# Another written-out order for an attention and feed-forward kernel, and its last output tile in parts of 384 and 128 columns

## The chip, the cores and the metric

The kernel runs on one NeuronCore of a Trainium2 chip. The metric is the device time of one execution in microseconds (us), as the median of several runs. One further execution is recorded by the hardware profiler; the lines and durations in this text come from it. The core has five engines that work side by side, each through its own queue in order: TensorE (PE; its weight loads are shown as PEld), VectorE (DVE), ScalarE (ACT), GpSimd (POOL) and SyncE (SP). DMA transfers are issued from the queues of POOL, SP and ScalarE.

## The reference

Attention over 8 batches and 8 heads, with 576 tokens and a head dimension of 64. In front of the keys and values stand 16 "beacon" keys and values which every query sees; the others are causal. Then a gated feed-forward network without a nonlinearity follows over all 4608 tokens:

```
scores = 0.125 * q @ concat(beacon_k, k).T      # masked above the diagonal
a      = exp(scores - max) / sum
x      = (a @ concat(beacon_v, v)) as 4608 tokens x 512
out    = ((x @ w1) * (x @ w2)) @ w3 @ w_out     # 512 -> 1024 -> 1024 -> 512
```

## The kernel before, in words

All products are in fp16 with fp32 sums. Since nothing nonlinear stands between `w3` and `w_out`, the kernel multiplies these two first (`Wt`, 1024 x 512) and so needs one output product instead of two.

There are no loops in the program that set the order of the work. A text, `ORDER`, lists every step; a short loop reads it and calls one small function for each entry. Each engine gets its instructions in the order of that list, and semaphores hold an instruction until its data is there and its buffer is free. So a step's place in the list is its place in the queue of its engine, and a step that waits holds everything behind it on that engine. The entries, with the lines of the profile:

- Loads, nearly all on POOL's queue (letter P; S is SP's queue, A is ScalarE's): `lq b c` and `lk b c` load queries and keys of batch b (chunk c of 128 rows; for batch 0, head pair c; lines 331, 339, 356), `lv` and `lvb` values and beacon values (339, 384), `lkb` beacon keys, `l1` and `l2` quarters of the two up-projections (389), `l3` an eighth of `w3` (398), `lo` a quarter of `w_out` (401). Up to eight loads are under way; a ninth waits for the oldest to land.
- Transposes of q and k: `tq`, `tk` on TensorE (421 for batch 0, 427 for others) with `eq`, `ek` copying the result out of PSUM; batch 0 first has its rows put in order by `cast`. Most of the later batches use transposing loads on SP instead, `Dq` and `Dk` (470, 476). `tn`, `en` do it for batch 0's beacon keys.
- The weight product: `t3 r` transposes an eighth of `w3` (483), `e3` copies it out, `f r a` multiplies (492), `ew` copies `Wt` out.
- Attention: `s b g` computes a group of score blocks (507; 13 groups a batch, K = 64 rows, two heads at once), `exp` exponentiates it on ScalarE (517, 128 x 1024, 1.03 us), `m` masks diagonal blocks on VectorE, `v b t h` multiplies with the values (538), `n` divides by the row sum on VectorE (549, 550).
- Turning x: `x b i` on TensorE (564) with the copy `ex`, or the transposing DMA `TX b i` on SP (573).
- Feed-forward, in 9 chunks of 512 tokens: `a mc kf` and `b mc kf` (579, four products of 512 columns each), copied or multiplied by `ea` and `eb`; `o mc mt` the output product of 128 tokens (600, eight products), `eo` scales it out of PSUM, `st` stores it (614).
- `spin n` runs n products of zeros on TensorE, to fill waits at the start. `consts` sets up constants.

A letter A or D in a copying step says whether ScalarE or VectorE does it; the number beside it is the PSUM bank. `o`, `eo` and `st` may carry a first column and a width, with which a tile is made in parts.

Two functions matter for the tail:

```
def eo(mc, mt, e, n, c0=0, w=DM):
    i = slot["st", (mc, mt)] if c0 else take("st", (mc, mt), NST)
    scaled(e, sts[i][:, ds(c0, w)], bank(n)[:, 0:w], float(1.0 / GS))
```

and `st`, which issues the store of these columns from the named queue. The whole order, before and after, is in the listing and in the diff.

Of the kernel before, what the change touches and what calls it, by code (L numbers as in the profile page):

```python
# [696 lines left out]
```

## Time and profile before

| | |
|---|---|
| median of 5 runs | 292.66 us (291.24 to 293.65) |
| the profiled execution | 292.49 us |
| its span, first to last instruction | 289.7 us |
| TensorE busy | 283.6 us (98%), 2904 matmuls |
| VectorE, ScalarE, POOL busy | 171.6, 147.3, 134.2 us |
| first matmul, first transpose, last matmul's end | 1.26, 5.99, 286.60 us |
| DMA moved | 38.85 MB, mean 134 GB/s |

The profile's page shows the busy time of each engine, the same in 40 slices of the span, the DMA queues, the chain of work that ended last, and the costliest groups of instructions with what ended the idle time before them. Other views of the trace show stages of the span, the chain in order of time, the waits, and the instructions in order of time. "Landing" is when a DMA's data is reported complete. A matmul is pipelined, so the price of one is read from start to start, not from its shown duration.

### The profile page before, as it was taken

How to read it: one execution, taken by the hardware profiler on the slowest of the kernel's cores; microseconds unless marked ns; L12 is line 12 of the kernel's file. 1: busy time of each engine (PE TensorE's matmuls, PEld its weight loads, DVE VectorE, ACT ScalarE, POOL GpSimd, SP SyncE). 2: the span in 40 equal slices, each digit the busy share in tenths (PEclk: the TensorE clock that was granted, in tenths of full speed). 3: DMA queues.
4: the chain of work that ended last, by engine and by line, in shares of the span. 5: the costliest groups of instructions: out<-in, count | busy, mean ns of one | idle time of the engine just before them, and what ended most of it. 6: DMA issues, size and time to landing. Idle time of an engine off the chain costs nothing.

```text
span 289.7 us, 7032 instructions
## 1 busy us (share of the span) xinstructions
PE 283.6 (98%) x2904; PEld 153.6 (53%) x2904; DVE 171.6 (59%) x370; ACT 147.3 (51%) x188; POOL 134.2 (46%) x187
## 2 busy tenths in 40 slices
PE   7999999999999999999999999999999999999995
PEld 3446675565565655565544555555555445444443
DVE  4244586885586856665563566575766565676710
ACT  3677779646574754678125656646473153000022
POOL 8769898798668651285396464450010011000000
PEclk9999999999999999999999999999999999999999
DMA  9999999999999999499999999997121005300033
GB/s 156 202 200 176 172 172 178 171 156 146 165 189 142 144 157 227 104 133 178 159 156 154 178 203 104 154 191 161 35 69 38 36 36 151 78 2 0 0 145 145
DMA packets 154318, 38.85 MB, mean 134 GB/s; under 512 B 144112, under 2 KB 150000, under 8 KB 154288
## 3 DMA queue, kind: packets, MB, share of 16 engines
q0 software_dynamic: 114800, 26.46, 104.7%
q1 hardware_dynamic: 39280, 11.68, 25.0%
q8 instruction: 22, 0.36, 0.5%
q10 hardware_dynamic: 208, 0.29, 0.4%
q14 instruction: 8, 0.07, 0.1%
HBM read 39.32 MB, written 9.44 MB: 168 GB/s over the span
## 4 chain that ended last, share of the span: by engine, by line
PE 86%; DMA 7%; POOL 5%; issue 1%; ACT 0%; POOLq 0%
PE one L579 44%; PE one L600 22%; PE one L538 10%; PE pair L507 8%; DMA q<-in_q_dram 2%; DMA st<-in_k_dram 2%; DMA wo<-in_moe_w_out_dram 2%; POOL va L339 2%; PE one L564 1%; POOL xT L398 1%; PE one L427 1%; POOL q L331 1%; PE one L492 1%; POOL k L339 1%; POOL w L389 0%
## 5 line engine op out<-in xcount | busy, mean ns | idle before, releaser
L579 PE MATMUL one<-xT,w 128*128 128x512 f16 x576 | 133.6, 379 | 0.0
L517 ACT ACTIVATE ring<-pair 128x1024 f16<-128x1024 f32 x104 | 99.3, 1028 | 21.2 <-PE pair L507 19.2
L579 PEld LDWEIGHTS <-w 128*128 128x128 f16 x576 | 53.0, 98 | 59.3 <-issue 2.7
L600 PE MATMUL one<-Wt,gT 128*128 128x512 f16 (+1 forms) x296 | 66.5, 374 | 0.0
L594 DVE TENSOR_TENSOR gT<-one,asb 128x512 f16<-128x512 f32 x72 | 49.1, 689 | 23.2 <-PE one L579 16.3
L299 ACT ACTIVATE asb<-one 128x512 f32<-128x512 f32 x32 | 19.2, 600 | 75.4 <-PE one L579 51.0
L614 POOL DMA_DIRECT2D out_dram<-st x27 | 15.3, 569 | 66.9 <-DVE st L301 29.6
L339 POOL DMA_DIRECT2D va<-in_v_dram x40 | 33.9, 851 | 21.8 <-PE one L538 15.6
L600 PEld LDWEIGHTS <-gT 128*128 128x128 f16 x296 | 27.7, 98 | 30.7 <-issue 1.3
L538 PEld LDWEIGHTS <-ring 128*128 128x128 f16 x960 | 35.2, 97 | 10.0 <-issue 1.0
L538 PE MATMUL one<-va,ring 128*128 128x65 f16 x960 | 37.8, 193 | 0.0
L301 DVE TENSOR_SCALAR asb<-one 128x512 f32<-128x512 f32 x40 | 27.5, 689 | 14.7 <-PE one L579 14.0
L339 POOL DMA_DIRECT2D k<-in_k_dram x35 | 29.8, 857 | 10.8 <-DMA kT<-k 6.7
L550 DVE TENSOR_TENSOR x<-one,rd 128x384 f16<-128x384 f32 (+1 forms) x64 | 31.4, 491 | 2.2
L331 POOL DMA_DIRECT2D q<-in_q_dram x35 | 30.0, 865 | 5.7 <-DMA va<-in_v_dram 3.1
L507 PE MATMUL pair<-qT,kT 64*128 64x80 f16 (+4 forms) x736 | 30.6, 225 | 0.1
L507 PEld LDWEIGHTS <-kT 64*128 64x128 f16 x736 | 19.7, 95 | 14.4 <-issue 11.9
L299 ACT ACTIVATE st<-one 128x512 f32<-128x512 f32 (+1 forms) x18 | 10.3, 574 | 24.3 <-PE one L600 23.9
L527 DVE TENSOR_TENSOR ring<-ring,MD 128x768 f16<-128x768 f16 x32 | 17.7, 552 | 7.9 <-ACT ring L517 7.9
L301 DVE TENSOR_SCALAR st<-one 128x512 f32<-128x512 f32 x19 | 13.1, 690 | 14.1 <-PE one L600 14.1
L527 DVE TENSOR_TENSOR ring<-ring,MX 128x384 f16<-128x384 f16 x32 | 11.3, 354 | 16.1 <-ACT ring L517 16.1
L549 DVE RECIPROCAL rd<-one 128x6 f32<-128x6 f32 (+1 forms) x64 | 11.7, 183 | 12.5 <-PE one L538 12.2
(63 smaller groups left out, 134.1 us busy)
## 6 DMA issues: line engine op xcount, KB each, us to landing
out_dram<-st POOLq DMA_DIRECT2D x27, 256.0 KB, 6.6
q<-in_q_dram POOLq DMA_DIRECT2D x28, 128.0 KB, 6.3
va<-in_v_dram POOLq DMA_DIRECT2D x24, 128.0 KB, 6.9
k<-in_k_dram POOLq DMA_DIRECT2D x21, 128.0 KB, 6.7
xT<-in_moe_w_dram POOLq DMA_DIRECT2D x8, 256.0 KB, 6.3
w<-in_moe_w_dram POOLq DMA_DIRECT2D x8, 256.0 KB, 7.3
out_dram<-st SPq DMA_DIRECT2D x8, 256.0 KB, 2.0
wo<-in_moe_w_out_dram POOLq DMA_DIRECT2D x4, 256.0 KB, 6.4
```

Of the source, the lines that this page charges most:

```text
L299: nc.scalar.activation(dst, src, AF.Copy, scale=by)
L301: nc.vector.tensor_scalar(dst, src, by, None, ALU.mult)
L331: nc.gpsimd.dma_start(dst[:rows, c], src[b, :, ds(c * P, rows), :].rearrange("h s d -> s h d"))
L339: nc.gpsimd.dma_start(dst[ds(p0, rows), c], src[b, :, ds(s0, rows), :].rearrange("h s d -> s h d"))
L507: nc.tensor.matmul(shape(n, "pair")[:, hh, ds(col, w)], kT[ds(hh * 64, 64), t, ts(jt, P)], qT[ds(hh * 64, 64), t, ds(q0, w)],)
L517: nc.scalar.activation(held(b, g)[:, :, 0:GW], shape(n, "pair"), AF.Exp, scale=scale)
L527: nc.vector.tensor_tensor(blk, blk, msk, ALU.mult)
L538: nc.tensor.matmul(pv[:, 2 * at + hh, 0 : D + 1], held(b, g)[:, hh, ds(col, P)], va[:, jt, 2 * t + hh, 0 : D + 1], start=(jt == 0), stop=( ...
L550: nc.vector.tensor_tensor(x16s[b % NB2][:, ds(2 * h, ni), ts(t, P)].rearrange("p i (h d) -> p i h d", h=2), pv[:, 0 : 2 * ni, 0:D].rearran ...
L579: nc.tensor.matmul(bank(n), w12[:, kt, ds(i * DF + kf * P, P)], xT[:, kt, ds(mc * 512, 512)], start=(kt == 0), stop=(kt == NKT - 1),)
L594: nc.vector.tensor_tensor(gTs[mc % 2][:, kf, :], bank(n), asb[slot["asb", (mc, kf)]], ALU.mult)
L600: nc.tensor.matmul(bank(n)[:, 0:w], gTs[mc % 2][:, kf, ts(mt, P)], Wt[:, kf, ds(c0, w)], start=(kf == 0), stop=(kf == NFT - 1),)
```

## The change

Only the text `ORDER` changes; all functions stay. 1190 entries become 1191. What differs:

- The first part, batch 0 and the weight product up to about the first scores of batch 1, is in another order: other eighths of `w3` first, scores after the first group later and products `f` earlier, the loads in an accordingly different order, other banks, and other choices between ScalarE and VectorE. The two loads outside POOL's queue swap queues.
- The rest has the same steps in a similar sequence, with differences in order, banks and engines throughout. In batch 7, tile 0 is turned by `x` and `ex` (TensorE, ScalarE) where it was a `TX` (SP). 22 output tiles instead of 19 are scaled by VectorE (with the last half tile's move among them), and 11 instead of 10 stores are issued by SP.
- The last output tile (8,0) is made as 384 columns and then 128, instead of 256 and 256; the last part is scaled by VectorE instead of ScalarE.

The diff, cut to the start, the turn to batch 1, a stretch of batch 2, one of batch 7 and the end:

```diff
 ORDER = """
-consts 0; lq 0 0 S; lk 0 0 A; l3 6; consts 1; spin 8 7; lq 1 2 P; l3 4; lo 1; lkb 0 P;
-cast 0 0 q A; lo 0; cast 0 0 k D; lkb 1; consts 2; spin 2 7; tq 0 0 6; tk 0 0 7; eq 0 0 D 6;
-lq 0 1 P; ek 0 0 A 7; spin 1 0; t3 6 5; lk 0 1 P; e3 6 A 5; spin 1 6; tq 1 2 6; l3 3; eq 1 2 A 6;
-spin 3 7; t3 4 7; lvb 0; e3 4 D 7; lo 2; spin 3 6; tn 0 6; en 0 A 6; lk 1 0 P; spin 1 7; s 0 0 0;
-s 0 1 2; s 0 2 4; exp 0 0 0; f 6 0 7; l3 0; f 4 0 6; lk 0 2 P; exp 0 2 4; m 0 0 0; f 6 1 7;
-cast 0 1 q D; lo 3; f 4 1 6; cast 0 1 k D; exp 0 1 2; tq 0 1 5; lk 0 3 P; tk 0 1 4; ek 0 1 D 4;
-eq 0 1 A 5; spin 1 0; t3 3 3; lq 0 3 P; m 0 0 1; l3 5; s 0 3 0; s 0 4 4; e3 3 D 3; exp 0 3 0;
-f 6 2 7; lvb 1; f 3 0 3; exp 0 4 4; m 0 1 0; l3 2; s 0 5 0; tk 1 0 2; f 3 1 3; exp 0 5 0; t3 0 5;
-lq 0 2 P; f 3 2 3; e3 0 D 5; ek 1 0 A 2; lk 1 1 P; f 4 2 6; cast 0 2 k A; m 0 1 1; f 0 0 4;
-f 0 1 4; lv 0 4; f 0 2 4; f 6 3 7; cast 0 3 k A; l3 1; f 0 3 4; ew 6 D 7; lv 0 0; tk 0 3 5;
-ew 0 A 4; f 4 3 6; cast 0 3 q D; ek 0 3 A 5; tq 0 3 7; ew 4 D 6; t3 5 4; lv 1 0; eq 0 3 A 7;
-f 3 3 3; e3 5 D 4; lv 0 2; tk 0 2 6; ew 3 A 3; t3 2 7; ek 0 2 A 6; lv 0 3; f 5 0 5; e3 2 D 7;
-f 5 1 5; cast 0 2 q A; lv 0 1; f 5 2 5; f 5 3 5; lq 1 3 P; tq 0 2 6; ew 5 D 5; tk 1 1 7;
-eq 0 2 A 6; f 2 0 4; l1 2; ek 1 1 D 7; s 0 6 0; s 0 7 2; l3 7; exp 0 6 0; t3 1 6; lq 1 1 P;
-f 2 1 4; e3 1 D 6; f 2 2 4; exp 0 7 2; lq 1 4 P; f 2 3 4; m 0 2 0; lq 1 0 P; f 1 0 7; ew 2 A 4;
-f 1 1 7; lk 1 2 P; f 1 2 7; f 1 3 7; lk 1 3 P; v 0 1 0 6; ew 1 A 7; v 0 2 0 5; n 0 1 0 6; tq 1 3 4;
-lk 1 4 P; v 0 0 0 7; n 0 2 0 5; eq 1 3 A 4; s 0 8 0; n 0 0 0 7; v 0 0 1 6; exp 0 8 0; lv 1 3;
-s 0 9 2; s 0 10 4; s 0 11 0; n 0 0 1 6; exp 0 9 2; l1 0; t3 7 7; m 0 2 1; v 0 1 1 6; e3 7 D 7;
-exp 0 11 0; lv 1 1; tq 1 1 3; tq 1 4 2; n 0 1 1 6; f 7 0 7; eq 1 4 A 2; l2 0; f 7 1 7; exp 0 10 4;
-m 0 3 0; s 0 12 0; m 0 3 1; lq 2 1 P; v 0 3 0 6; eq 1 1 D 3; tk 1 2 2; exp 0 12 0; v 0 2 1 5; l1 1;
-n 0 3 0 6; f 7 2 7; n 0 2 1 5; ek 1 2 A 2; lv 1 2; x 0 4 6; x 0 0 4; v 0 3 1 3; ex 0 4 A 6;
-ex 0 0 D 4; l2 1; f 7 3 7; n 0 3 1 3; tq 1 0 6; lv 1 4; tk 1 4 5; tk 1 3 4; eq 1 0 D 6; ek 1 4 A 5;
-x 0 2 3; x 0 3 2; lq 2 0 P; ek 1 3 D 4; ex 0 2 A 3; x 0 1 6; ex 0 3 D 2; s 1 0 0; s 1 1 4; s 1 2 2;
-ex 0 1 A 6; lv 2 0; ew 7 D 7; exp 1 0 0; a 0 0 6; l2 2; b 0 0 7; exp 1 2 2; m 1 0 0; ea 0 0 D 6;
-lk 2 0 P; s 1 3 0; s 1 4 2; exp 1 1 4; eb 0 0 7; tq 2 1 6; a 0 1 7; eq 2 1 D 6; l1 3; exp 1 3 0;
-m 1 0 1; b 0 1 6; l2 3; ea 0 1 D 7; exp 1 4 2; m 1 1 0; s 1 5 4; s 1 6 0; s 1 7 2; eb 0 1 6;
...
-lq 2 4 P; exp 1 9 4; m 1 2 1; a 0 6 7; ea 0 7 D 6; lkb 3; Dk 2 0; exp 1 10 2; s 1 11 0; s 1 12 4;
...
-ek 2 1 A 3; ex 1 0 D 4; lk 3 2 P; ex 1 4 D 5; v 1 2 1 7; eb 0 5 2; Dq 2 4; tq 2 2 5; lk 3 1 P;
...
-lk 4 3 P; eq 2 3 D 2; Dq 3 2; lq 3 0 P; eo 0 2 D 7; s 2 0 0; s 2 1 4; s 2 2 2; exp 2 0 0; lk 4 0 P;
...
-TX 7 0; exp 7 12 2; v 7 2 1 7; eo 6 1 D 6; TX 7 4; o 6 2 5; n 7 2 1 7; st 6 1 P; v 7 3 1 7;
...
-o 7 3 7; eo 7 2 D 6; st 7 2 S; o 7 0 6; eo 7 3 A 7; st 7 3 S; o 8 3 7; eo 7 0 A 6; st 7 0 S;
-o 7 1 6; eo 8 3 A 7; st 8 3 S; o 8 2 7; eo 7 1 A 6; st 7 1 S; o 8 0 6 0 256; eo 8 2 A 7; st 8 2 S;
-eo 8 0 A 6 0 256; st 8 0 S 0 256; o 8 0 5 256 256; eo 8 0 A 5 256 256; st 8 0 S 256 256
+consts 0; lk 0 0 S; lq 0 0 A; l3 4; consts 1; spin 8 7; lo 1; lkb 0 P; l3 6; lo 0; l3 2;
+cast 0 0 k A; lq 0 2 P; consts 2; cast 0 0 q A; spin 2 7; tk 0 0 6; l3 1; ek 0 0 D 6; spin 1 7;
+tq 0 0 7; lo 2; t3 4 5; eq 0 0 D 7; e3 4 D 5; l3 0; spin 2 6; tn 0 6; en 0 A 6; lk 0 1 P; spin 1 7;
+s 0 0 0; s 0 1 2; s 0 2 4; exp 0 0 0; lq 0 1 P; t3 6 6; e3 6 D 6; exp 0 1 2; spin 2 7; f 4 0 7;
+lo 3; m 0 0 0; f 4 1 7; exp 0 2 4; m 0 0 1; f 6 0 6; lk 0 2 P; t3 2 3; f 6 1 6; e3 2 D 3; lvb 1;
+cast 0 2 q D; spin 1 0; f 2 0 5; f 2 1 5; lv 1 0; t3 1 4; tq 0 2 3; e3 1 A 4; f 6 2 6; eq 0 2 D 3;
+lvb 0; f 2 2 5; f 1 0 4; lk 1 0 P; spin 2 3; t3 0 3; f 1 1 4; e3 0 A 3; cast 0 1 k D; lkb 1;
+f 1 2 4; tk 0 1 2; cast 0 1 q D; lv 0 4; f 4 2 7; ek 0 1 A 2; tq 0 1 3; f 0 0 2; eq 0 1 A 3; l3 5;
+s 0 3 0; cast 0 2 k A; l3 3; f 4 3 7; lv 0 1; f 1 3 4; ew 4 D 7; exp 0 3 0; tk 0 2 3; f 0 1 2;
+lk 0 3 P; ek 0 2 D 3; f 0 2 2; ew 1 A 4; lk 1 1 P; tk 1 0 7; m 0 1 0; f 0 3 2; ek 1 0 A 7;
+lq 0 3 P; f 2 3 5; ew 0 D 2; f 6 3 6; lq 1 2 P; ew 2 A 5; t3 5 7; ew 6 D 6; lv 0 2; s 0 4 0;
+s 0 5 2; s 0 6 4; e3 5 A 7; t3 3 6; lv 0 0; exp 0 4 0; f 5 0 7; e3 3 D 6; f 5 1 7; lv 0 3; f 5 2 7;
+exp 0 6 4; cast 0 3 k D; f 5 3 7; lk 1 2 P; tk 0 3 6; exp 0 5 2; m 0 2 0; s 0 7 0; l3 7;
+ek 0 3 D 6; tk 1 1 5; f 3 0 4; lv 1 3; exp 0 7 0; m 0 1 1; f 3 1 4; tq 1 2 6; cast 0 3 q D; l1 2;
+f 3 2 4; ek 1 1 A 5; eq 1 2 D 6; f 3 3 4; lk 1 4 P; ew 5 A 7; tq 0 3 6; ew 3 D 4; lq 1 4 P;
+eq 0 3 A 6; lq 1 1 P; v 0 2 0 5; v 0 0 0 7; lq 1 0 P; n 0 2 0 5; s 0 8 2; n 0 0 0 7; v 0 0 1 6;
+lq 1 3 P; exp 0 8 2; s 0 9 0; s 0 10 4; n 0 0 1 6; lk 1 3 P; exp 0 9 0; tk 1 2 7; t3 7 3; m 0 2 1;
+lv 1 2; v 0 1 0 6; ek 1 2 D 7; e3 7 A 3; v 0 1 1 2; m 0 3 0; n 0 1 0 6; v 0 3 0 7; lq 2 1 P;
+exp 0 10 4; s 0 11 0; n 0 3 0 7; f 7 0 6; l1 0; n 0 1 1 2; tq 1 4 3; exp 0 11 0; s 0 12 4;
+v 0 2 1 7; lv 1 1; eq 1 4 D 3; exp 0 12 4; x 0 0 2; m 0 3 1; tq 1 1 3; l2 0; f 7 1 6; ex 0 0 D 2;
+f 7 2 6; eq 1 1 D 3; lq 2 0 P; tq 1 0 5; n 0 2 1 7; v 0 3 1 4; l2 1; tq 1 3 3; eq 1 0 D 5; f 7 3 6;
+eq 1 3 A 3; n 0 3 1 4; lv 1 4; x 0 4 7; tk 1 4 5; tk 1 3 2; ew 7 A 6; l2 3; ek 1 4 D 5; x 0 3 3;
+x 0 2 4; ek 1 3 D 2; ex 0 3 A 3; x 0 1 6; l2 2; ex 0 2 D 4; s 1 0 0; s 1 1 2; s 1 2 4; ex 0 1 A 6;
+ex 0 4 D 7; exp 1 0 0; tq 2 1 7; l1 1; a 0 1 6; eq 2 1 D 7; exp 1 2 4; lk 2 0 P; m 1 0 0; a 0 0 7;
+ea 0 1 D 6; exp 1 1 2; s 1 3 0; s 1 4 4; ea 0 0 D 7; l1 3; b 0 0 6; exp 1 3 0; m 1 0 1; lv 2 0;
...
+eb 0 2 4; ea 0 3 A 7; s 1 8 0; s 1 9 2; s 1 10 4; lq 2 4 P; exp 1 8 0; eb 0 3 6; a 0 6 7; lk 3 4 P;
+Dk 2 0; exp 1 9 2; m 1 2 1; a 0 7 6; lv 2 2; ea 0 6 D 7; exp 1 10 4; s 1 11 0; s 1 12 2; lq 3 4 P;
...
+b 0 6 4; ek 2 2 A 6; n 1 3 1 2; Dq 2 4; b 0 5 6; lvb 2; eb 0 6 4; v 1 2 1 5; lk 3 2 P; Dk 3 4;
...
+lk 3 3 P; ex 1 2 D 2; s 2 0 0; s 2 1 4; s 2 2 2; eo 0 2 D 6; exp 2 0 0; a 1 3 7; st 0 2 P;
...
+n 7 3 0 7; v 7 3 1 6; TX 7 4; eo 6 3 A 3; x 7 0 7; n 7 3 1 6; o 6 2 5; st 6 3 S; ex 7 0 A 7;
+TX 7 2; a 7 0 6; eo 6 2 D 5; TX 7 1; b 7 0 7; st 6 2 S; ea 7 0 D 6; TX 7 3; b 7 3 5; eb 7 0 7;
...
+eb 7 2 7; ea 7 4 A 5; eb 7 4 3; o 7 2 6; eo 8 3 D 4; st 8 3 S; o 7 3 7; eo 7 2 D 6; st 7 2 S;
+o 7 1 6; eo 7 3 D 7; st 7 3 S; o 7 0 7; eo 7 1 D 6; st 7 1 S; o 8 2 6; eo 7 0 A 7; st 7 0 S;
+o 8 1 7; eo 8 2 D 6; st 8 2 S; o 8 0 6 0 384; eo 8 1 A 7; st 8 1 S; eo 8 0 A 6 0 384;
+st 8 0 S 0 384; o 8 0 5 384 128; eo 8 0 D 5 384 128; st 8 0 S 384 128
 """
```

## The prediction

> **What bounds the kernel now.** I read the page first, then the stages, then the chain of waits, then the last microseconds in the timeline. From the page:
>
> ```profile
> span 289.7 us, 7032 instructions
> PE 283.6 (98%) x2904; PEld 153.6 (53%) x2904; DVE 171.6 (59%) x370; ACT 147.3 (51%) x188; POOL 134.2 (46%) x187
> ...
> DMA  9999999999999999499999999997121005300033
> ...
> q8 instruction: 22, 0.36, 0.5%
> ...
> PE 86%; DMA 7%; POOL 5%; issue 1%; ACT 0%; POOLq 0%
> ```
>
> TensorE is busy 98%, and the chain is TensorE but for a DMA and POOL part. Where that part lies, the stages and the chain tell:
>
> ```profile
> 6.00:37.00 31.00, 29.58 (x367) 17.71 (x367) 14.79 (x32) 21.61 (x29) 25.87 (x39) 1.00 1.62 186
> 37.00:60.00 23.00, 23.00 (x336) 14.13 (x335) 18.00 (x44) 18.56 (x24) 19.39 (x26) 1.00 2.02 173
> ```
>
> (The stage; its length; busy time and instructions of PE, PEld, DVE, ACT, POOL; clock; DMA share; GB/s.)
>
> ```profile
> 12.25 6.83 DMA st<-in_k_dram
> 19.08 0.28 issue
> ...
> 29.89 6.84 DMA q<-in_q_dram
> 36.72 0.05 issue
> 36.77 0.29 PE one L427 x4
> ...
> 72.09 0.77 PE pair L507 x22
> 72.86 1.83 PE one L600 x8
> ...
> 76.47 1.73 PE one L600 x8
> ...
> 272.76 13.85 PE one L600 x72
> ```
>
> Until 36.72 us the chain is the line of loads on POOL's queue; from 36.77 us it never leaves TensorE. So the end is "a landing, plus all TensorE work listed after what needed it", and a change of order helps only by earlier landings or more work listed before them. A small cost is visible too: eight products take 1.73 us, but 1.83 right after score products.
>
> **The ruler.** TensorE's steady prices, from start to start in the trace: `a` or `b` 0.863 us, `o` 1.727, `f` 0.432, `t3` 0.458, a spin 0.216, a batch-0 transpose op 0.256, others 0.223 (less where rows are fewer), `v` 0.548 or 0.368, `s` 0.221 to 0.236, and 0.182 for each unbroken group of `s` (0.095 entering, 0.087 leaving). Before: work 266.66 + 20 spins 4.32 + 41 groups 7.46 = 278.44 us. The last matmul ends at 286.60 us; less 0.17 for its own drain, some 8.0 us are lost. The loss (start in the trace minus list up to there) is 3.8 at the first transpose (5.99 us), 4.8 at 11 us, 6.5 at 24.3, 7.31 at 36.77, 7.35 at 43.4, 7.7 at 58, and 8.0 at the end.
>
> **The change, part by part.**
>
> *TensorE's list.* After: 266.85 + 19 spins 4.10 + 42 groups 7.64 = 278.59. One more `x` (batch 7, tile 0; 4 transposes of 112 columns, 0.198) replaces a transposing DMA, one spin less (-0.216), one more group (+0.182): **+0.15 us**, all on the path. The last tile's 384 + 128 columns stream as many as 256 + 256.
>
> *The line of loads.* All land in order. Clean steps between landings are 1.21 to 1.25 us for `l3` and `lo`, 0.72 to 0.77 for batch 0's q and k, about 0.85 for a later chunk (0.6 for its fifth), 0.7 to 0.9 for `lv`, 1.31 for `l1`/`l2`, 0.17 for a beacon. I do not add these up from zero; I swap sets against a landing of before. (1) `lq 1 4` landed at 36.72 as the 35th POOL load. After, it is the 36th: one `lv` and one fifth chunk more, one full chunk less, +0.8 + 0.6 - 0.85 = +0.55, so 37.27. The list before its transposes counts 29.99 us (before: 29.46): loss 37.32 - 29.99 = 7.33, against 7.31. (2) The first up-projection `a 0 1` needs `l1 0`, the 43rd load. The 43rd of before, `l2 0`, landed at 43.96; the sets differ by a chunk in place of a 1.31 weight load, -0.46, so 43.50. List before it: spins 4.10, `f` 13.82, `t3` 3.66, transposes 4.58, scores with groups 5.35, `v` 3.66, `x` 1.01 = 36.18; loss 43.55 - 36.18 = 7.37, against 7.35 at the same place. Same price, same line: **0.0**, with -0.4 if the start is denser (before, the second and third landings came 1.16 and 1.39 apart where clean steps are 0.85 and 1.23; after, the second is a `lo`, whose issue takes 0.56 us and not 0.94) and +0.7 if one more of the late landings falls in. Late landings exist: the load that landed at 19.08 came 1.44 after its predecessor, its neighbours of the kind 0.72 to 0.77, and a 16 KB packet of the instruction queue started at 16.89. Three such packets before 39 us, 0.3 to 0.7 each, are in the landings I swap against.
>
> The Trainium skill's page "Runtime: NRT & Kernel Launch" (Instruction fetch mechanics) says an instruction buffer is refilled in 16 KiB blocks of 256 instructions and the cost of crossing a block is mostly hidden. By that, planning around fetches gains 0; by the 1.44 us row it could gain 0.7 a packet, and measurement wins on that.
>
> *Batch 0's evacuations.* Eight `eq`/`ek` more go to VectorE (0.42 or 0.76 for 0.59 or 0.64 us on ScalarE), three of eight `e3` to ScalarE (1.01 for 0.69), a cast to VectorE (0.39 for 0.83). Both first casts now stand on ScalarE, so the second first transpose waits until about 6.8 us instead of 6.25; at that place the loss is 4, and the load line asks for 7.3 later, so it costs nothing. Summed up to the first scores of batch 1, ScalarE goes from 28.7 to 26.7 us and VectorE from 23.9 to 26.4, under 42.5 us of time: no new bound. The thin place is the turn to batch 1. Counted from the end of `v 0 3 1`: `n` ends at 1.0 us, `ek 1 4` at 1.35, `ek 1 3` at 1.77, for scores that start at 1.9; ScalarE's `eq`, `ew`, `ex 0 3`, `ex 0 1` end at 2.7, for `a 0 1` at 2.87. Cover 0.1 us each; if it goes, 0.3 to 0.6 us, of which the wait for `l1 0` hides 0.2. Taken: 0.
>
> *After 43 us.* The score groups stand at the same places in the list within about 2 us throughout. Before lost 0.65 us there, in waits of 0.1 or less; I take the same, with 0 and +1 as ends. The thinnest cover of before: the transposing load `Dq 2 4`, issued at 61.64 when `lq 2 4` landed (61.57), landed at 68.45, 0.10 before batch 2's first scores. After, one `lv` less stands ahead, so it lands 0.8 earlier for scores at the same 60.8 us of list: cover 0.9. The store of tile (6,2) now waits on SP ahead of `TX 7 3`, about 2.6 us; that tile is needed 9.5 us of list after its release, and landed 2.5 us after issue in this stretch. No cost.
>
> *The tail.*
>
> ```profile
> 285.51 1.87 SPq L614 DMA_DIRECT2D out_dram<-st  x3
> 285.81 0.38 ACT L299 ACTIVATE st<-one 128x256 f32<-128x256 f32 x1 [0.33 <-PE one L600]
> 286.63 0.38 ACT L299 ACTIVATE st<-one 128x256 f32<-128x256 f32 x1 [0.44 <-PE one L600]
> ```
>
> ```profile
> out_dram<-st SPq DMA_DIRECT2D x8, 256.0 KB, 2.0
> out_dram<-st SPq DMA_DIRECT2D x2, 128.0 KB, 1.7
> ```
>
> Before, with T the last matmul's end: copy to T+0.41, issue, landing at T+2.15, then 0.92 us of closing. After: the 384 columns end at T-0.45; ScalarE's copy, between its 0.384 (256) and 0.597 (512), takes 0.49, to T+0.06; its 192 KB land by T+1.95. VectorE's copy of 128 columns, by its PSUM rows (0.424 for 256, 0.557 for 384), takes 0.29, to T+0.31, but SP's first issue holds the queue 0.33 us and its wait: issue T+0.46, and 1.56 us for 64 KB (1.7 to stay on the row): T+2.02 to T+2.17. **-0.13** (0.0 to -0.25).
>
> The page "VectorE: DVE Perf Modes" (Specifications) places ScalarE closer to PSUM, which speaks against VectorE here; its cycle table gives 0.26 against 0.25 us for 128 columns, so by it, too, nothing but the overlap matters.
>
> Sum: +0.15 + 0.0 + 0.0 - 0.13 = **0.0 us**. The profiled execution is 292.49 us (span 289.7 and 2.8 around it), the median of the runs 292.66; I predict **292.6 us**, its own range 291.5 to 293.7.
>
> **Rivals.**
> *The load line is denser (faster).* For: the looser start of before (0.45 us) and its late landings. If 0.4 of start and two late landings (0.7 each) vanish, the loss at `a 0 1` is 7.37 - 1.8 = 5.6; but the turn's covers and `lq 1 4` are only relieved as far as their own work allows, so I count 1.0 to 1.8: 291.0 us. Against: as many instructions, so as many packets; the same bytes at the same 186 GB/s.
> *`l1 0` lands late (slower).* It is the last load needed with nothing to spare; `lq 2 1` was put ahead of it. Each us later than 43.5 moves all 242 us of list behind it by one. Two more late landings, 1.4 us, and the lost cover of the turn, 0.4: 294.4. It decides from a landing at about 45.0. Against: in before no load that TensorE waited for after 36.8 us cost more than 0.1.
> *The cover of `Dq 2 4` goes.* Transposing loads took up to 9.21 us at 70 to 90 us. At 9.2 instead of 6.8 it lands 1.5 late: 294.1.
> *The change does nothing it says:* the tail gains 0 since SP serialises, and the start gains 0; 292.7, inside the forecast.
>
> **Chances.** Forecast (within 0.5%, 1.46 us, about what a measurement here can tell from no change) 0.56; denser line 0.21; late `l1 0` 0.14; `Dq 2 4` and its like 0.09. A denser line mostly gives 291.0 and so counts as faster. Leaving one in ten on each side: 290.5 to 294.9.
>
> **What would show it.** Right: after's chain of waits leaves DMA at 36.5 to 44 us and stays on TensorE; TensorE x2907; the span after the last matmul about 2.9 to 3.1 us; `a 0 1` starting at 43.2 to 43.9. Wrong: a DMA in the chain after 45 us, `a 0 1` off by over 1 us, or more than 0.3 us of waits for ScalarE or VectorE between 40 and 44 us.

## The result, and the profile after

The changed kernel takes 293.4 us (median of 37 runs, 291.98 to 295.28); the kernel before, run beside it, 291.83 us (72 runs). The medians lie 1.57 us apart; the ratio of the means, which I go by, is 1.0045 with a 95% interval of 1.0034 to 1.0056: slower by 1.3 us. That lies inside the half per cent that I had called "no change", and 293.4 lies inside the stated range, but the sum of the prediction was a change of zero, and the interval leaves zero out. That the time itself fell into the range is in part luck: the prediction starts from 292.66 us, the median of five runs of before, and that of all 72 is 0.83 us lower.

The page of the kernel after, with the same lines as shown of before (span; busy time; DMA share in 40 slices; the instruction queue; the chain's shares):

```profile
span 290.8 us, 7036 instructions
...
PE 283.7 (98%) x2907; PEld 153.6 (53%) x2907; DVE 173.6 (60%) x374; ACT 146.6 (50%) x185; POOL 133.7 (46%) x186
...
DMA  7999999999999999999999995999330014200034
...
q8 instruction: 22, 0.36, 0.5%
...
PE 84%; DMA 10%; POOL 5%; issue 1%; DVE 0%; POOLq 0%
```

TensorE's busy time grew by 0.1 us, as its list did; the span grew by 1.1. The chain has 10% DMA instead of 7%. The stages (length; busy time of PE, PEld, DVE, ACT, POOL; clock; DMA share; GB/s):

```profile
6.00:37.00 31.00, 28.87 (x360) 17.77 (x361) 16.95 (x35) 19.66 (x25) 24.41 (x37) 1.00 1.58 180
37.00:60.00 23.00, 22.63 (x327) 13.59 (x324) 17.88 (x45) 17.31 (x22) 19.27 (x25) 1.00 2.03 173
```

Between 6 and 37 us TensorE is busy for 0.71 us less than before and the DMA rate is 180 GB/s, not 186; another 0.37 us is missing between 37 and 60. The chain in order of time (start, length, what):

```profile
3.98 6.69 DMA wo<-in_moe_w_out_dram
10.67 0.28 issue
10.95 8.72 DMA wo<-in_moe_w_out_dram
19.68 0.28 issue
19.96 1.11 POOL xT L399 x2
...
25.02 6.74 DMA va<-in_v_dram
31.75 0.28 issue
...
38.46 6.24 DMA w<-in_moe_w_dram
44.70 0.05 issue
44.75 1.90 PE one L580 x8
```

The chain leaves the DMAs at 44.75 us, with the first up-projection `a 0 1`, where before it left them at 36.77. It goes from landing to issue to landing: 0.28 us after a load has landed, POOL issues the next one, and that one is what the next step waits for. (Lines of the kernel after are one higher: L580 was L579, L399 was L398.) What TensorE waited for, longest first, apart from the constants at the start:

```profile
PE one L422 <- DVE o16k L296: 0.8, 1, 0.8
PE one L539 <- DMA va<-in_v_dram: 0.5, 1, 0.5
PE one L580 <- DMA w<-in_moe_w_dram: 0.3, 1, 0.3
```

In the terms of the prediction, the loss (start in the trace less TensorE's list up to there), read at the same times, of the two kernels and of some experiments that follow:

| kernel | 12 us | 20 | 28 | 30 | 34 | 38 | 44 | 46 | 60 | 270 |
|---|---|---|---|---|---|---|---|---|---|---|
| before | 4.84 | 5.54 | 6.61 | 6.63 | 6.92 | 7.42 | 7.35 | 7.35 | 7.70 | 7.98 |
| after | 4.84 | 5.54 | 6.06 | 7.05 | 7.97 | 7.98 | 8.08 | 8.56 | 8.75 | 8.93 |
| after, small loads apart (e1) | 5.27 | 6.00 | 6.17 | 6.18 | 7.05 | 7.20 | 7.26 | 7.94 | 8.03 | 8.21 |
| e1 with a spin less (e15) | 5.98 | 6.42 | 6.78 | 6.79 | 7.20 | 7.32 | 7.38 | 8.15 | 8.24 | 8.42 |
| before, small loads together (e5) | 5.20 | 7.01 | 7.73 | 7.87 | 8.56 | 8.83 | 8.95 | 8.95 | 9.42 | 10.29 |
| before, loads as needed (e10) | 4.36 | 4.94 | 5.83 | 5.83 | 5.97 | 6.08 | 6.21 | 6.32 | 6.56 | 7.70 |

After is ahead by 0.55 us at 28, then loses 0.97 at `tk 0 3` (28.75, its k tile landed at 27.99 and was still to be cast), 0.9 at the first value products (33.2), 0.25 at `tq 1 4` (38.2) and 0.46 at `a 0 1` (44.75, `l1 0` landed at 44.70). From there to the end it loses 0.4, less than before (0.6). So the whole cost shows between 28 and 45 us, all of it at steps that wait for a landing, at `tk 0 3` by way of the cast.

**Where the landings went.** The issues on POOL in that stretch (start, length, what; in brackets the idle time before and what ended it):

```profile
12.21 0.64 POOL L357 DMA_DIRECT2D st<-in_k_dram  x1 [0.69 <-DMA xT<-in_moe_w_dram]
...
14.20 0.84 POOL L340 DMA_DIRECT2D va<-in_v_dram  x1 [0.67 <-DMA xT<-in_moe_w_dram]
15.45 0.53 POOL L385 DMA_DIRECT2D va<-in_beacon_v_dram  x1 [0.42 <-DMA wo<-in_moe_w_out_dram]
16.71 0.83 POOL L340 DMA_DIRECT2D k<-in_k_dram  x1 [0.73 <-DMA xT<-in_moe_w_dram]
...
19.96 1.11 POOL L399 DMA_DIRECT2D xT<-in_moe_w_dram  x2 [0.77 <-DMA wo<-in_moe_w_out_dram]
```

POOL waits for a landing before it can issue: eight loads are under way, and a ninth needs the oldest to have landed. When `lo 3` landed at 19.68, the seven behind it were `lk 0 2`, `lvb 1`, `lv 1 0`, `lvb 0`, `lk 1 0`, `lkb 1` and `lv 0 4`. Three of them are beacons of 16 KB. By their clean steps (0.77, 0.17, 0.85, 0.17, 0.77, 0.17, 0.6) they are 3.5 us of transfer; in before no seven loads behind another came to less than 5.1 from the sixth load on. The next load was issued at 19.96, and 3.5 us of stock is less than it takes a load from issue to landing. From the trace's landings (us):

| load of after | issued | landed | since the landing before | clean step | issue to landing |
|---|---|---|---|---|---|
| `lo 3` | 10.95 | 19.68 | 1.77 | 1.21 | 8.72 |
| `lvb 0` | 15.45 | 21.06 | 0.26 | 0.17 | 5.61 |
| `lk 1 0` | 16.71 | 21.71 | 0.64 | 0.77 | 5.00 |
| `lv 0 4` | 18.46 | 22.34 | 0.44 | 0.6 | 3.88 |
| `l3 5` | 19.96 | 23.61 | 1.26 | 1.24 | 3.64 |
| `l3 3` | 20.52 | 25.55 | 1.94 | 1.24 | 5.03 |
| `lv 0 1` | 21.06 | 27.11 | 1.55 | 0.8 | 6.05 |

Issue to landing shrinks to 3.64 us: the queue has run dry. Then two landings come 0.7 us late each. The rate points the same way: the stretch from 20.5 to 25.5 us in after, and below it the same stretch of before:

```profile
20.50:25.50 5.00, 4.82 (x54) 2.84 (x54) 3.10 (x5) 3.88 (x7) 5.00 (x8) 1.00 1.46 159
```

```profile
20.50:25.50 5.00, 4.50 (x47) 2.70 (x46) 2.85 (x5) 4.07 (x7) 4.57 (x6) 1.00 1.52 190
```

159 GB/s against 190, while POOL is busy issuing for all of the 5.00 us. The two stretches do not carry the same loads, though: by the clean steps a chunk of 128 KB moves at about 154 GB/s and an `l3` of 256 KB at about 213, and after has more chunks there. The fair comparison is the same loads in another order, which is the first experiment. I call this the hole in the line of loads: it is my theory of the 1.3 us. The rivals were the cast moved to VectorE (the longest single wait in the list above), the new tail, and the instruction packet of 16 KB that started at 17.32 us and made `lo 3` land 0.5 us late.

The tail of after (the timeline, and the last stores' KB and us from issue to landing):

```profile
285.00 3.63 SPq L615 DMA_DIRECT2D out_dram<-st  x4
...
287.30 0.49 ACT L300 ACTIVATE st<-one 128x384 f32<-128x384 f32 x1 [0.70 <-PE one L601]
287.75 0.29 DVE L302 TENSOR_SCALAR st<-one 128x128 f32<-128x128 f32 x1 [2.78 <-PE one L601]
```

```profile
out_dram<-st SPq DMA_DIRECT2D x1, 192.0 KB, 1.9
out_dram<-st SPq DMA_DIRECT2D x1, 64.0 KB, 1.7
```

With T the last matmul's end, the last store was issued at T+0.53 and landed at T+2.21 (before: T+0.45 and T+2.15); the program ended at T+3.12 (T+3.08). The copy took 0.29 us as estimated, but the small store landed no sooner than one of twice its size: 1.68 against 1.71 us.

### The profile page after: what moved, and what is told of

Its sections match the earlier page's. It is cut to its first block, busy times and chain, and to the rows that moved or that the text cites. A ratio compares the mean times of both kernels' runs of the same rounds, so it can differ in the third digit from the quotient of the medians.

```text
span 290.8 us, 7036 instructions
## 1 busy us (share of the span) xinstructions
PE 283.7 (98%) x2907; PEld 153.6 (53%) x2907; DVE 173.6 (60%) x374; ACT 146.6 (50%) x185; POOL 133.7 (46%) x186
## 4 chain that ended last, share of the span: by engine, by line
PE 84%; DMA 10%; POOL 5%; issue 1%; DVE 0%; POOLq 0%
PE one L580 44%; PE one L601 22%; PE one L539 9%; PE pair L508 8%; DMA wo<-in_moe_w_out_dram 5%; DMA va<-in_v_dram 2%; DMA w<-in_moe_w_dram 2%; POOL q L332 2%; PE one L565 1%; POOL xT L399 1%; POOL k L340 1%; POOL va L340 1%; POOL st L357 0%; PE one L428 0%; POOL b L369 0%
## 5 line engine op out<-in xcount | busy, mean ns | idle before, releaser
L580 PE MATMUL one<-xT,w 128*128 128x512 f16 x576 | 133.9, 379 | 0.3 <-DMA w<-in_moe_w_dram 0.3
L580 PEld LDWEIGHTS <-w 128*128 128x128 f16 x576 | 52.4, 98 | 59.7 <-issue 3.6
L601 PE MATMUL one<-Wt,gT 128*128 128x512 f16 (+2 forms) x296 | 66.2, 373 | 0.0
L300 ACT ACTIVATE asb<-one 128x512 f32<-128x512 f32 x37 | 22.2, 600 | 65.7 <-PE one L580 46.8
L302 DVE TENSOR_SCALAR asb<-one 128x512 f32<-128x512 f32 x35 | 24.1, 688 | 15.8 <-PE one L580 15.7
L302 DVE TENSOR_SCALAR st<-one 128x512 f32<-128x512 f32 (+1 forms) x22 | 14.8, 673 | 19.0 <-PE one L601 18.9
L300 ACT ACTIVATE st<-one 128x512 f32<-128x512 f32 (+1 forms) x15 | 8.9, 595 | 28.9 <-PE one L601 27.5
```

Source lines behind the costliest of these rows:

```text
L300: nc.scalar.activation(dst, src, AF.Copy, scale=by)
L302: nc.vector.tensor_scalar(dst, src, by, None, ALU.mult)
L580: nc.tensor.matmul(bank(n), w12[:, kt, ds(i * DF + kf * P, P)], xT[:, kt, ds(mc * 512, 512)], start=(kt == 0), stop=(kt == NKT - 1),)
L601: nc.tensor.matmul(bank(n)[:, 0:w], gTs[mc % 2][:, kf, ts(mt, P)], Wt[:, kf, ds(c0, w)], start=(kf == 0), stop=(kf == NFT - 1),)
```

## The experiments

Ratios are to the kernel before, run on the same chip beside each, with 95% intervals. Executions of one program differ in the start: the loss at 12 us is 4.84 in both profiles above and 4.4 to 6.0 in those that follow. So profiles are compared from 12 us on.

### Is it the hole? Small loads apart (e1), and the hole put into the kernel before (e5)

The kernel after, with the two beacon-value loads taken out of the cluster:

```diff
-e3 2 D 3; lvb 1; cast 0 2 q D;
+e3 2 D 3; cast 0 2 q D;
...
-eq 0 2 D 3; lvb 0; f 2 2 5;
+eq 0 2 D 3; f 2 2 5;
...
-lv 0 2; s 0 4 0;
+lv 0 2; lvb 0; s 0 4 0;
...
-lv 1 3; exp 0 7 0;
+lv 1 3; lvb 1; exp 0 7 0;
```

> The changed kernel with only the two 16 KB loads of beacon values (lvb 1, lvb 0) moved down POOL's queue: behind lv 1 3 and behind lv 0 2. Nothing that TensorE does before 32 us reads them, and together they transfer for 0.34 us. Theory 1 (a hole in the line of loads: eight loads may be under way, and between 16 and 21 us of the changed kernel four of the eight are small, so that the line runs dry while POOL waits for a slot): the steps of 1.94 us (l3 3) and 1.55 us (lv 0 1) shrink to about 1.25 and 0.8, l1 0 lands 0.8 to 1.0 us earlier than 44.70, the first a 0 1 starts as much earlier, and the time is 0.7 to 0.9 us shorter than that of the changed kernel: ratio to before about 1.001 to 1.002. Theory 2 (evacuations on other engines and the other order of products cost the time): l1 0 lands within 0.3 us of 44.70 and the ratio stays at 1.004 to 1.005.

Measured: 292.4 us, ratio 1.0015 [0.9991, 1.0040]. `l3 3` now landed 1.26 us after its predecessor and `lv 0 1` 0.90, both as clean as in before, and `l1 0` landed at 43.98, 0.72 earlier than in after although this execution started 0.43 later. The rate in the same stretch of the line (0.5 us later, with the start):

```profile
21.00:26.00 5.00, 5.00 (x60) 3.08 (x59) 3.10 (x5) 4.16 (x7) 5.00 (x8) 1.00 1.62 188
```

188 GB/s for nearly the same loads, and TensorE busy for all of it. An instruction packet hit `lo 3` here too (17.77 us; 1.88 us after its predecessor), so the packet is not what made the difference. From 12 to 46 us this kernel loses 2.67 us; after lost 3.72, before 2.51.

The other way round, the kernel before with four small loads put together:

```diff
-cast 0 0 k D; lkb 1; consts 2;
+cast 0 0 k D; consts 2;
...
-lk 1 0 P; spin 1 7;
+lk 1 0 P; lkb 1; lvb 0; lvb 1; lkb 2; spin 1 7;
```

(`lvb 0`, `lvb 1` and `lkb 2` leave their later or earlier places.)

> The kernel before with only four 16 KB loads gathered on POOL's queue: lkb 1, lvb 0, lvb 1 and lkb 2 stand together behind lk 1 0. Nobody needs them sooner or later than they land in either case, and lkb 2 alone adds 0.17 us of transfer ahead of what follows. The seven loads behind lo 2 then take 3.5 us to transfer (before: 6.8), as the seven behind lo 3 do in the changed kernel, where the line ran dry. Theory 1 (hole when the seven behind take less than about 4 us): landing steps of 1.9 where 1.24 is clean between 16 and 22 us, the loss at 37 us 0.5 to 1.1 us larger than before's 7.31 by the same start, ratio 1.002 to 1.004. Theory 2 (the small loads were innocent, only bytes count): +0.17 us, ratio 1.0005.

Measured: 295.01 us, ratio 1.0110 [1.0079, 1.0141], far more than expected. The seven loads behind `lo 2` are again 3.5 us of transfer; issue to landing fell from 7.41 to 4.52 us, and `l3 0` landed 1.92 us after its predecessor, `l3 5` 1.54, where both are clean at 1.24. The chain in order of time shows the same alternation as after's:

```profile
8.33 7.41 DMA wo<-in_moe_w_out_dram
15.74 0.28 issue
...
18.59 6.92 DMA xT<-in_moe_w_dram
25.50 0.28 issue
...
29.34 7.66 DMA xT<-in_moe_w_dram
37.00 0.28 issue
...
42.24 8.17 DMA w<-in_moe_w_dram
```

The hole alone, without any other part of the change, makes the kernel before slower. From 12 to 46 us e5 loses 3.75 us and before 2.51: 1.2 us more, as much as the hole in after. Most of it falls at `t3 0`, 1.45 us, which waits for `l3 0`; but that place is not the hole's alone, since an instruction packet started at 16.57 us, and in e9 below, which has no hole, one at 16.59 met `l3 0` and cost 1.48 us there. After 46 us later transfers lost their cover too, 0.7 us more than in before: `lq 2 4` landed at 64.29 instead of 61.57 and its transposing load then held up batch 2's first scores (0.41 us). The end was 0.3 us later (T+3.35), with a packet at T-1.92. The rest of the 3.2 us is not accounted for.

### Is it the cast? (e4)

```diff
-cast 0 3 k D;
+cast 0 3 k A;
```

> The changed kernel with only the reordering copy of batch 0's last keys (cast 0 3 k) on ScalarE instead of VectorE, the engine it had before; TensorE waited 0.97 us for it at 28.75. Theory 1 (landings set the path): that wait changes by up to 0.5 us either way, since the copy starts with the landing of lk 0 3 at 27.99 all the same, but the next landings (lv 0 3 at 32.92, l1 0 at 44.70) absorb the difference; ratio to before stays 1.004 to 1.005. Theory 2 (the choice of engine costs the time): 0.4 to 0.9 us shorter than the changed kernel, ratio 1.001 to 1.003.

Measured on the kernel after: 293.06 us, 1.0035 [1.0014, 1.0055]. It stays slower, and with the cast on ScalarE TensorE still lost 0.76 us at `tk 0 3`. In e1, with the cast on VectorE, `lk 0 3` landed at 26.97 instead of 27.99, and nothing was lost there. So the late `lk 0 3` made the wait, not VectorE. The hole itself is at its plainest in e4's profile, in the microsecond in which `l3 5` was issued:

```profile
21.00:22.00 1.00, 0.71 (x15) 0.53 (x15) 0.00 (x0) 0.69 (x2) 0.79 (x3) 1.00 0.65 42
```

42 GB/s: next to nothing was left to transfer.

### Is it the tail? (e2, e9, e6, e7)

The kernel before with the new tail alone:

```diff
-o 8 0 6 0 256; eo 8 2 A 7; st 8 2 S;
-eo 8 0 A 6 0 256; st 8 0 S 0 256; o 8 0 5 256 256; eo 8 0 A 5 256 256; st 8 0 S 256 256
+o 8 0 6 0 384; eo 8 2 A 7; st 8 2 S;
+eo 8 0 A 6 0 384; st 8 0 S 0 384; o 8 0 5 384 128; eo 8 0 D 5 384 128; st 8 0 S 384 128
```

> The kernel before with only the last tile in 384 and 128 columns, the latter on VectorE. My prediction's term: the last store lands at 2.02 to 2.17 us after the last matmul's end (before: 2.15), 0.13 us gained, ratio 0.9995. Rival (SP issues one after the other, and a store of 64 KB lands no sooner than one of 128 KB): 2.15 to 2.25 us, ratio 1.000. In both the rest of the kernel does not move.

Measured: 292.81 us, 1.0027 [1.0006, 1.0048]. That was not expected. In its profile the program ended at T+3.94 and not T+3.12. And yet the kernel after with the old tail was no faster, nor was e1 with the old tail any slower (e6, e7; both undo the six entries above):

> The changed kernel with the last tile in 256 and 256 columns, both on ScalarE, as before; all else as changed. The tail alone in the kernel before was 1.0027 (1.0006 to 1.0048). Theory A (that was the draw of those runs; the tail is worth 0.0 to 0.2 us): ratio 1.0035 to 1.005, like the changed kernel. Theory B (the tail itself costs 0.3 to 0.8 us, since two stores are issued 0.43 us apart instead of 0.82 and the last one lands later): ratio 1.001 to 1.003.

Measured: 293.91 us, 1.0058 [1.0040, 1.0077].

> The changed kernel with the two 16 KB loads moved apart as in e1 and the last tile in 256 and 256 columns on ScalarE. Theory A (tail worth 0.0 to 0.2 us): as e1, ratio 1.000 to 1.002. Theory B (the tail costs 0.3 to 0.8 us): 0.998 to 1.000. If hole and tail together are all that the change did to the time, what remains is the 0.15 us of TensorE's list.

Measured: 292.33 us, 1.0009 [0.9997, 1.0021].

The same kernel as e2, measured anew:

> The kernel before with only the tail of 384 columns on ScalarE and 128 on VectorE, the same kernel as in the run of the tail alone, measured anew. Theory A (from after with the old tail, 1.0058, and the spread version with the old tail, 1.0009: the tail costs nothing): ratio to before 0.999 to 1.001. Theory B (the tail does cost something, as its first measurement had it): 1.002 to 1.004, with the last store landing 2.1 us or more after its issue.

Measured: 292.77 us, 1.0026 [1.0003, 1.0049], and again the end at T+3.93. So it belongs to this program, not to one execution. The last microseconds of e9 by DMA queue:

```profile
q14 instruction: 1, 0.01, 0.2%
issues: line engine op xcount, KB each, median us to landing
out_dram<-st SPq DMA_DIRECT2D x1, 64.0 KB, 2.4
```

A packet of 8 KB on an instruction queue started at T+1.66, just as the last store's packets went out. The store landed 2.43 us after its issue instead of 1.68; of its 128 packets of 512 bytes, eight, as many as one of the 16 DMA engines carries, started at T+2.14 to T+2.31, the others by T+1.86. I take the packet for VectorE's; the next experiments test that. In the kernel after the same packet came at T-2.30, where nothing waits for it; in before at T+3.7, after the end.

### When does the packet come? (e12, e13)

The trace records 448 instructions of VectorE in before, 450 in e2 and e9, 451 in after (those that do no work counted too). If the packet comes when VectorE's queue reaches a certain instruction, fewer instructions there move it past the end, more move it ahead. Two earlier copies off VectorE (e12), or one more on it (e13), both on the kernel of e2:

```diff
-ea 8 2 D 5;
+ea 8 2 A 5;
...
-ea 8 6 D 7;
+ea 8 6 A 7;
```

> The kernel before with the tail of 384 and 128 columns, and two earlier copies of up-projections in the last stretch (tile 8, rows 2 and 6) on ScalarE instead of VectorE, where ScalarE has been idle for over 10 us and TensorE waits for neither. Theory A (in the two profiles of the tail alone an 8 KB packet of instructions, fetched 1.6 us after VectorE's last copy began, falls into the last store and makes it land 2.43 us after its issue instead of 1.68; it comes when VectorE's instructions reach a certain number, so with fewer of them it comes after the end): last store landing 1.7 us after its issue, 3.1 to 3.2 us from the last matmul to the end, ratio to before 0.999 to 1.0005. Theory B (a 64 KB store behind VectorE's copy is slow in this order whatever is fetched): 3.9 us, ratio 1.0026 as in the two runs of the tail alone.

Measured: 292.55 us, 1.0018 [1.0003, 1.0033]. The packet came at T+3.72, and the store landed 1.74 us after its issue. Its last microseconds, with no instruction queue among the DMAs:

```profile
q1 hardware_dynamic: 303, 0.27, 27.9%
issues: line engine op xcount, KB each, median us to landing
out_dram<-st SPq DMA_DIRECT2D x1, 192.0 KB, 1.9
out_dram<-st SPq DMA_DIRECT2D x1, 64.0 KB, 1.7
```

The profile is as the theory of the packet said; the time, on its own, decides little, since its interval holds both ends. The end was still T+3.41 and not 3.1, since the closing after the last landing took 1.13 us (see the last section).

```diff
-eo 7 3 A 7;
+eo 7 3 D 7;
```

> The kernel before with the tail of 384 and 128 columns, and one copy of an output tile some 8 us before the end (tile 7, row 3) on VectorE instead of ScalarE. Theory A (the packet comes when VectorE's instructions reach a certain number): it now comes some 5 to 8 us before the last matmul's end, beside earlier stores that have time; 3.1 to 3.2 us from the last matmul to the end, ratio to before 0.9985 to 1.0005. Theory B (the store itself): 3.9 us, 1.0026.

Measured: 291.8 us, 1.0004 [0.9984, 1.0023]; the packet came at T-7.5, the store landed after 1.75 us, the end was T+3.26. The 64 KB store is not slow by itself.

### How much is the hole, with equal ends? (e15), and other orders of loads (e3, e8, e10, e14, e11)

e1's own end was T+3.67: a 16 KB packet of TensorE's instructions at T-1.83 delayed its last stores. Its last microseconds:

```profile
q8 instruction: 1, 0.02, 1.7%
q14 instruction: 1, 0.01, 0.4%
issues: line engine op xcount, KB each, median us to landing
out_dram<-st SPq DMA_DIRECT2D x2, 256.0 KB, 3.7
out_dram<-st SPq DMA_DIRECT2D x1, 192.0 KB, 2.4
out_dram<-st SPq DMA_DIRECT2D x1, 64.0 KB, 2.2
```

One spin less on e1:

```diff
-spin 8 7;
+spin 7 7;
```

> The kernel after with the small loads apart, and one spin of the first eight left out (0.22 us of work in a stretch where TensorE waits for loads). In the version with all spins a 16 KB packet of TensorE's instructions came 1.83 us before the last matmul's end, and the last store landed at 2.75 us after that end instead of 2.21. Theory A (the packet comes when TensorE's instructions reach a certain number; two fewer, one matmul and its weight load, move it past the end; and the hole in the line is all that made after slower): 3.1 to 3.2 us from the last matmul to the end, ratio to before 0.9990 to 1.0005. Theory B (the packet stays, or the hole is only a part of the loss): 3.6 us, ratio 1.001 to 1.002.

Measured: 292.23 us, 1.0010 [0.9988, 1.0032]. The packet moved to T+4.36, the last store landed after 1.67 us and the end was T+3.12, as said. The ratio lies between the two theories and settles nothing alone.

Five runs asked what a better order of loads can give. The kernel before with two loads that batch 1 needs late moved back:

```diff
-lv 1 0; eq 0 3 A 7;
+eq 0 3 A 7;
...
-l1 2; ek 1 1 D 7;
+ek 1 1 D 7;
...
-l2 0;
+l2 0; lv 1 0;
...
-l2 3;
+l2 3; l1 2;
```

> The kernel before with only two loads moved down POOL's queue: lv 1 0 (landed at 29.60, first read at 49.5 us) behind l2 0, and l1 2 (landed at 33.95, first read at 58.3) behind l2 3. Theory 1 (up to 44 us each landing on POOL's line passes to the end one for one): lq 1 4 lands about 2.0 us earlier than 36.72, l2 0 about 2.0 earlier than 43.96; what then binds is the landing of l3 2 and the transposes of batch 0 (loss 6.5 to 6.7 us by 28 us instead of 7.35), so the time falls by 0.5 to 0.7 us: ratio about 0.998. Theory 2 (the waits of TensorE for ScalarE and VectorE at this place take over): ratio 1.000, with TensorE waiting for evacuations between 30 and 44 us.

Measured: 291.98 us, 1.0002 [0.9981, 1.0023]. `lq 1 4` landed 1.8 us earlier, at 34.91, but the loss was already 7.18 at 25 us, ahead of the moved loads, and 0.52 came back at batch 2's first scores (69.6 us), which waited for a transposing load: `Dq 2 4`, the thin cover of the prediction.

Then all loads in the order of need, with the third chunk of batch 1's queries turned late:

```diff
-l3 6; lq 1 2 P; l3 4;
+l3 6; l3 4;
...
-tq 1 2 6; eq 1 2 A 6;
...
-lq 1 0 P;
+lq 1 0 P; lq 1 2 P;
...
-v 0 2 1 5; n 0 2 1 5;
+v 0 2 1 5; tq 1 2 3; n 0 2 1 5; eq 1 2 D 3;
```

(and `lkb 1` next to `lk 1 0`, `lv 1 0` behind `l2 0`, `l1 2` behind `l2 3`, and `lkb 3`, `lv 2 0`, `lv 2 3` behind `lq 2 4`.)

> The kernel before with loads put in the order of their need, and no hole (the seven behind never under 5.1 us): lq 1 2 and its transposes move from the start to beside lq 1 0 (0.85 to 1.16 us off the line for all that stands between); lv 1 0 behind l2 0, l1 2 behind l2 3 as in e3; lv 2 0, lv 2 3 and lkb 3 behind lq 2 4, whose transposed load batch 2's first scores waited 0.5 us for in e3; lkb 1 beside lk 1 0. Theory 1 (the line of loads sets the path until 69 us): the loss at 30 us falls from 6.63 to about 5.9, at 46 us from 7.35 to about 6.8, no wait at s 2 0 0, and the time falls by 0.5 to 0.8 us: ratio 0.997 to 0.998. Theory 2 (evacuations take over at once): 1.000.

Measured: 291.84 us, 0.9992 [0.9974, 1.0010]. Its first waits on TensorE were now for copies and casts rather than for loads:

```profile
PE one L421 <- ACT o16k L295: 0.5, 1, 0.5
PE one L421 <- ACT o16q L295: 0.3, 1, 0.3
```

So two of them were changed back:

```diff
-cast 0 3 k A;
+cast 0 3 k D;
...
-eq 1 2 D 3;
+eq 1 2 A 3;
```

> The kernel before with its loads in the order in which they are needed, as in the earlier run, and two evacuations changed back where that run showed TensorE waiting for them: the cast of the fourth k tile on VectorE (a wait of 0.63 us at its transposes), the copy of the third chunk of q of batch 1 on ScalarE (0.38 us at a v product). Theory A (the evacuations took what the loads gave back): up to 0.9 us less, ratio 0.996 to 0.998. Theory B (every engine's cover is equally thin there, so the wait moves to the next copy): 0.9985 to 1.0005, with waits for ACT or DVE copies of 0.3 us or more before 44 us still in the profile.

Measured: 291.46 us, 0.9976 [0.9957, 0.9994]: the one version that beat the kernel before, by 0.7 us, with 6.32 us of loss at 46 us against 7.35 (0.5 of it the start of this execution). A new wait of 0.84 us for a transposing load came at 92 us. Its end was T+3.40, again by a packet of TensorE's (T-1.82). With one spin less:

> The kernel before with its loads in the order of need and the two evacuations changed back, which measured 0.9976 with a 16 KB packet of TensorE's instructions 1.82 us before the last matmul's end and 3.40 us from that end to the program's; and one spin of the first eight left out. Theory A: the packet falls after the end, 3.1 us there, ratio 0.9960 to 0.9975. Theory B (the packet stays where it is, or the missing spin is paid by a later start): 0.9970 to 0.9985.

Measured: 291.72 us, 0.9983 [0.9964, 1.0003]. The end fell to T+3.08 as said, but no time was won: no faster than e10, within both intervals. In the profiled execution, a fetch packet at 16.53 us fell on `l3 0` (landing 2.77 us after its predecessor), and `t3 0` cost 1.78 us.

Last, the same idea on the kernel after: small loads apart, `lv 1 0` and `l1 2` later, the cast on ScalarE.

```diff
-lv 1 0; t3 1 4;
+t3 1 4;
...
-l1 2; f 3 2 4;
+f 3 2 4;
...
-cast 0 3 k D;
+cast 0 3 k A;
...
-lk 1 3 P; exp 0 9 0;
+lv 1 0; lk 1 3 P; exp 0 9 0;
...
-l2 1;
+l2 1; l1 2;
```

> The kernel after with the small loads apart (no seven loads behind another are shorter than 5.0 us before 44 us; 3.5 in after), and with two loads that batch 1 needs late moved behind what batch 0 needs (the first chunk of v of batch 1, 0.85 us, and the third up-projection weight, 1.31 us, so that the first weight lands some 1.3 us earlier than in the version with the small loads apart), and the cast of the fourth k tile on ScalarE. Theory A (the line of loads sets the loss up to the first up-projection): 0.7 to 1.3 us less than the version with the small loads apart, ratio to before 0.997 to 0.999. Theory B (as in the kernel before with its loads in the order of need: evacuations or a later load take the place): 0.9995 to 1.002.

Measured: 292.83 us, 1.0016 [0.9991, 1.0040]: a miss. `a 0 1` did not wait any more (`l1 0` landed at 43.06), but the cast on ScalarE cost 0.76 at `tk 0 3`, and the loads put behind the first weights took their place: 0.76 us at `a 0 2`, at 53.7 us, for `l1 1`. In the waits of TensorE:

```profile
PE one L422 <- ACT o16k L296: 1.5, 2, 0.9
...
PE one L580 <- DMA w<-in_moe_w_dram: 0.6, 1, 0.6
```

### What they say together

The end after T was the same in the one program that was profiled twice (3.94 and 3.93 in e2 and e9), so I take it off. The time over before is the ratio less one, times 292; the end is that of the profile, less 3.08:

| kernel | ratio | time over before | of it the end | rest |
|---|---|---|---|---|
| after | 1.0045 | +1.3 | 0.0 | +1.3 |
| after, old tail (e6) | 1.0058 | +1.7 | +0.2 | +1.5 |
| after, cast on ScalarE (e4) | 1.0035 | +1.0 | 0.0 | +1.0 |
| after, small loads apart (e1) | 1.0015 | +0.4 | +0.6 | -0.2 |
| the same, old tail (e7) | 1.0009 | +0.3 | +0.2 | +0.1 |
| the same, a spin less (e15) | 1.0010 | +0.3 | 0.0 | +0.3 |
| new tail on before (e2, e9) | 1.0027, 1.0026 | +0.8 | +0.9 | -0.1 |
| and packet moved (e12, e13) | 1.0018, 1.0004 | +0.5, +0.1 | +0.3, +0.2 | +0.2, -0.1 |

Each interval is worth 0.3 to 0.7 us either way, so single rows say little. But the three with the hole have a rest of 1.0 to 1.5 and the three without it -0.2 to +0.3, on average 1.2 us apart; and the loss from 12 to 46 us agrees: 3.72, 3.54 and 4.30 us with the hole (after, e6, e4), 2.67, 3.09 and 2.17 without (e1, e7, e15). The landings say it without the times of whole executions. Behind `lo 3`, up to `l1 0`, stand the same 30 loads in all six kernels; they took 25.02, 24.75 and 25.01 us with the hole, 23.76, 23.83 and 23.89 without. (In e6 `lv 0 2` came some 0.9 us late, with a packet at 29.16; that part may be the packet's.) The mean of the rests is good to about 0.5 us, so the hole is nearly all of the 1.3 us. Whether what ran short was loads under way or POOL's time to issue them (0.5 us even for a beacon that transfers in 0.17) was not separated. What is left fits the 0.15 us of TensorE's longer list, too small to be seen here.

## Why the prediction was right or wrong

**TensorE's list, +0.15: right.** 2907 matmuls, and the sum of its steady prices is 278.60 us against 278.45. No run tried it alone.

**The line of loads, 0.0: wrong, and this is the step that failed.** "I swap sets against a landing of before" compares which loads stand ahead of `l1 0`, and takes it that they land back to back in any order. That adds up bytes and leaves out the limit that the description of the loads names: eight under way, a ninth after the oldest has landed. `lq 1 4` landed at 38.17 where 37.27 was predicted, `l1 0` at 44.70 where 43.50 was, and `a 0 1` lost 8.55 us where 7.37 was predicted: 1.2 us, nearly all the miss. The sets themselves were counted rightly: with the small loads apart `l1 0` landed at 43.98 in e1, which started 0.43 later, so at 43.55 on after's clock. The number to compute was the transfer time of the seven loads behind each load, which needs nothing but the order and the clean steps that the prediction already listed: 3.5 us at `lo 3`. The loads that before issued between 8 and 25 us took 5.3 to 7.7 us from issue to landing; that includes waiting behind each other, and the least in the table above was 3.64.

**The slow rival had the place, not the mechanism.** "`l1 0` lands late" named the load and the step; its landing at 44.70 fell just short of the threshold of about 45.0. It was priced by two more late landings, of the kind that the prediction put down to instruction packets; in fact the packets were as many as before (22), and between 15 and 20 us one hit on each side (`lk 0 2` before, `lo 3` after). Of the listed signs of error one was met, `a 0 1` off by 1.2 us; the chain left the DMAs at 44.75, past the 44 of "right" and short of the 45 of "wrong".

**Instruction fetches, 0 by the page and up to 0.7 a packet by the row: the row was nearer.** The Trainium skill's "Runtime: NRT & Kernel Launch" (Instruction fetch mechanics) calls the cost of crossing a block mostly hidden. Here the loads that single packets hit landed 0.5 to 1.5 us late, which cost TensorE as much as 1.5 us at `t3 0` in e9, and packets cost 0.3 to 0.9 us at the end of the program.

**Batch 0's evacuations, 0: half right.** The turn to batch 1 showed no wait of ScalarE's or VectorE's, as argued. One cast upstream was exposed (0.8 us at `tk 0 3` in the list of waits); e4 and e1 show that the late load, not the engine, set it.

**After 43 us, the same 0.65: right, a little pessimistic.** After lost 0.4 there. The cover of `Dq 2 4` held in after; it went in e3 and e5, where the line was disturbed, as the third rival had it.

**The tail, -0.13: it came out at +0.04, just beyond the upper end of its bracket, 0.** The 0.29 us of the copy was right, and that SP serialises the two issues too (T+0.53, not T+0.46). The landing is the term that was mis-sized: 1.68 us for 64 KB where 1.56 was taken. What the step had no term for is the packet that the moved copy can pull into the last store: 0.75 us in e2 and e9, 0 in after.

## What to carry to other kernels

Where a queue keeps a fixed number of loads under way, an order is not only a sum of bytes: behind each load, add the transfer times of those that may be under way with it, and keep small loads spread out, not in a cluster. In these kernels, with eight under way, a sum of 3.5 us starved the line and one of about 5 did not; where between the two it begins was not tried. A change of which load stands where is best judged by the first step that waits for a landing, and then by the covers behind it, since taking back one wait mostly uncovers the next (e3, e8, e11). And read the last microseconds of a trace for instruction packets before crediting or blaming a change to the tail: moving one instruction to another engine can move a fetch (e12, e13).
